# Batch 0's norms in a fused attention and MLP kernel: transposed scores, inverse norms on ScalarE, squares summed on VectorE

## The chip, the cores and the metric

One NeuronCore of a Trainium2 chip. The metric is the device time of one execution in microseconds (us), as the median of several runs; lower is better. The engines are TensorE (PE in the profile; its weight loads are PEld), VectorE (DVE), ScalarE (ACT), GpSimd (POOL), which issues most loads here, and SyncE (SP).

## The reference

Two steps. The first is an attention over channels: for each of 4 batches, q and k (6080 rows, 256 channels) are scaled so that each channel has norm 1 over its rows; the 256x256 matrix of scores is their product over the rows, a softmax goes over it, and v is multiplied by the result. The second is an MLP with a squared relu.

```python
B, N, C = (4, 6080, 256)            # q, k, v; float32
qn = q / (norm(q, axis=1) + 1e-06)
kn = k / (norm(k, axis=1) + 1e-06)
s = kn.transpose(0, 2, 1) @ qn / tau          # tau = 1
a = softmax(s, axis=-1)                       # (sum + 1e-9 below)
x = (v @ a).reshape(24320, 256)
r = maximum(x @ w_in, 0)                      # w_in: 256 x 2048
out = (s_moe * r * r + b_moe) @ w_out         # w_out: 2048 x 256, out float32
```

## The kernel before

Everything is in fp16 with fp32 sums. The kernel forms `wa = a @ w_in` for each batch (a 256x2048 matrix), so that the main stream is `h = wa^T v^T`, relu, square, and the product with `w_out`. The main stream runs over groups of 512 rows, 16 steps each; the scores of the next batch are formed in small pieces between its steps. Batch 0 has no stream to hide behind: its q and k are loaded, its scores, norms and softmax are done, and only then does the stream begin.

The rows of a batch come in chunks of up to 512 rows (128 partitions, JC = 4 rows each). For batch 0 there are 11 chunks of 512 and two short ones (256 and 192 rows); the k rows of the two short ones are loaded before their q rows.

```python
    def mm(self, c, j):                       # the Gram product of q and k
        ...
            po(nc.tensor.matmul(
                self.s_ps[:, ch, :],
                kc[:np_, j, ts(ch, P)],
                qc[:np_, j, :],
        ...
    def norm_ops(self, c):
        # squares of k on ScalarE, of q on VectorE, then two folds on VectorE:
        #   4 rows to 2 (128x1024 out), 2 rows to 1 (128x512 out)
        ...
            if last and (self.b == 0 or c == 0 or c == len(self.chunks) - 1):
                for rows in self.rows:
                    rows.append((st["f", half], np_, 1))
        ...
        def into_first():                     # later batches: a DMA adds the fold to chunk 0's
            dst, src = self.rows[0][0][0][:np_], st["f", 1][:np_]
            po(nc.gpsimd.dma_start(out=dst, in_=src, accum_op=ALU.add))
        ...
    def add_norms(self, arrays=(0, 1), last=False):
        # sums over the partitions: products of 128x128 pieces of the folds with a column of ones
        ...
                po(nc.tensor.matmul(self.n_ps[a][:, ch : ch + 1], t[:np_, a, j, ts(ch, P)],
                                    ones16[:np_, 0:1], ...))
```

From the sums to the softmax (`finish_ops`): a root as exp(0.5 ln), an added eps and a reciprocal; then in batch 0 a scaling of the scores by k's inverse norm, a transpose on TensorE in fp32, and the exps with q's inverse norm as scale. In later batches the scaled scores are split into two fp16 halves, transposed by DMA and joined.

```python
        def root(out, sums):
            po(nc.scalar.activation(out=out, in_=sums, func=AF.Ln, bias=tiny))
            po(nc.scalar.activation(out=out, in_=out, func=AF.Exp, scale=0.5))
        def recip(a=None):
            ...
            po(nc.vector.tensor_scalar_add(out=nrm, in0=nrm, scalar1=EPS))
            po(nc.vector.reciprocal(out=r, in_=nrm))
        def scale():                          # batch 0
            for ch in range(CH):
                po(nc.vector.tensor_scalar_mul(
                    out=st["s"][:, ch], in0=self.s_ps[:, ch],
                    scalar1=st["r"][:, 1, ch : ch + 1]))
        def split(part): ...                  # later batches: "hi", "lo", each with two DMA transposes
        def join(): ...
        def turn(): ...                       # batch 0: nc.tensor.transpose with ident32
        def exps(j):
            po(nc.scalar.activation(
                out=st["e"][:, j, :], in_=st["t"][j], func=AF.Exp,
                scale=st["r"][:, 0, j : j + 1]))
```

The opening, in program order. Fillers (`keep_busy`) are products whose result nobody reads; they keep TensorE's activity up between the loads.

```python
    FILL = {-9: 2, -8: 2, -7: 2, -6: 4, -5: 4, -4: 4, -3: 2}     # 128x512 fp16 each
    for c in range(NCH0 - 2):
        ops = g0.norm_ops(c)
        if c >= NCH0 - 3:
            g0.add_norms()
        for j in range(g0.chunks[c][2]):
            g0.mm(c, j)
        ...                                   # fillers, then the squares and folds
    ops = [g0.norm_ops(c) for c in (NCH0 - 2, NCH0 - 1)]
    g0.add_norms()
    for k_squares, _, into_rows in ops:
        k_squares()
        into_rows()
    fin[0]()                                  # k's norm
    fin[1]()                                  # k's reciprocal
    keep_busy(NFILL, ...)
    for c in (NCH0 - 2, NCH0 - 1):
        ops[c - NCH0 + 2][1]()                # q's squares
        for j in range(g0.chunks[c][2]):
            g0.mm(c, j)
    ...                                       # q's norm, scaling, reciprocal, transpose
    transpose_v(0)
    keep_busy(2, w_in16[:, 0, :P], w_in16[:, 0, :NW])
    for f in fin[6:12]:                       # exps, row sums, first pieces of wa
        f()
```

Of the kernel before, what the change touches and what calls it, by code (L numbers as in the profile page):

```python
# [16 lines left out]
def kernel(  # L17
# [32 lines left out]
    SHIFT = 3  # L50
    assert CH == 2 and FT == 16
# [14 lines left out]
    sq_pool = pool("sq_pool", 2)  # L66
    f3_pool = pool("f3_pool", 13)
# [41 lines left out]
    class Gram:  # L109
# [32 lines left out]
        def mm(self, c, j):  # L142
            qc, kc = self.tiles[c]
            _, np_, jc = self.chunks[c]
            for ch in range(CH):
                po(nc.tensor.matmul(  # L146
                    self.s_ps[:, ch, :],
                    kc[:np_, j, ts(ch, P)],
                    qc[:np_, j, :],
                    start=(c == 0 and j == 0 and ch == 0),  # L150
                    stop=(c == len(self.chunks) - 1 and j == jc - 1 and ch == CH - 1),
                    skip_group_check=True,
                ))

        def norm_ops(self, c):
# [4 lines left out]

            def squares(a, js):
                def f():
                    if "sq" not in st:
                        st["sq"] = sq_pool.tile([P, 2, JC, C], FP16, tag="sq", name="sq")
                    if a == 0:
# [7 lines left out]
            def fold(half, arrays, last):  # L173
                def f():
# [10 lines left out]
                    if last and (self.b == 0 or c == 0 or c == len(self.chunks) - 1):  # L185
                        for rows in self.rows:
                            rows.append((st["f", half], np_, 1))
                return f

            def into_first():  # L190

                dst, src = self.rows[0][0][0][:np_], st["f", 1][:np_]
                po(nc.gpsimd.dma_start(out=dst, in_=src, accum_op=ALU.add))  # L193

            def unfolded():
                for rows in self.rows:
                    rows.append((st["sq"], np_, jc))
# [5 lines left out]
            if jc == 2:  # L203
# [4 lines left out]
            return ops + [into_first] if self.b > 0 and 0 < c < len(self.chunks) - 1 else ops  # L208

        def add_norms(self, arrays=(0, 1), last=False):  # L210

            if self.b > 0:

                self.n_all = x_tile[0][:, 1, : 2 * CH].rearrange("p (a c) -> p a c", a=2)
                self.n_ps = [self.n_all[:, 0], self.n_all[:, 1]]
            for a in arrays:
                first = self.n_ps[a] is None
                if first:
                    self.n_ps[a] = ps_o.tile([P, 2, C], FP32, tag="o_ps", name="n_ps")[:, 0, :CH]
                todo = [(t, np_, j, ch) for t, np_, jc in self.rows[a] for j in range(jc)  # L220
                        for ch in range(CH)]
                self.rows[a].clear()
                for i, (t, np_, j, ch) in enumerate(todo):
                    po(nc.tensor.matmul(self.n_ps[a][:, ch : ch + 1], t[:np_, a, j, ts(ch, P)],
                                        ones16[:np_, 0:1], start=(first and i == 0),
                                        stop=(last and i == len(todo) - 1),
                                        skip_group_check=True))

        def finish_ops(self):
# [3 lines left out]
            def root(out, sums):  # L233

                po(nc.scalar.activation(out=out, in_=sums, func=AF.Ln, bias=tiny))
                po(nc.scalar.activation(out=out, in_=out, func=AF.Exp, scale=0.5))

            def norms(a=None):

                if "r" not in st:  # L240
                    st["nrm"] = sm_pool.tile([P, 2, CH], FP32, tag="nrm", name="nrm")
                    st["r"] = sm_pool.tile([P, 2, CH], FP32, tag="rnrm", name="rnrm")
                if a is None:
                    self.add_norms(last=True)
                    root(st["nrm"], self.n_all)
                else:
                    self.add_norms((a,), last=True)
                    root(st["nrm"][:, a], self.n_ps[a])

            def recip(a=None):  # L250
                own = slice(0, 2) if a is None else slice(a, a + 1)
                nrm, r = st["nrm"][:, own], st["r"][:, own]
                po(nc.vector.tensor_scalar_add(out=nrm, in0=nrm, scalar1=EPS))
                po(nc.vector.reciprocal(out=r, in_=nrm))
                if inv_tau != 1.0 and a != 1:
                    po(nc.vector.tensor_scalar_mul(
                        out=st["r"][:, 0], in0=st["r"][:, 0], scalar1=inv_tau))

            def scale():
                st["s"] = sm_pool.tile([P, CH, C], FP32, tag="sm_s", name="sm_s")  # L260
                for ch in range(CH):
                    po(nc.vector.tensor_scalar_mul(
                        out=st["s"][:, ch], in0=self.s_ps[:, ch],
                        scalar1=st["r"][:, 1, ch : ch + 1]))


            def split(part):
                st[part] = sm_pool.tile([P, CH, C], FP16, tag=f"s_{part}", name=f"s_{part}")
                rk = st["r"][:, 1]
                if part == "hi":  # L270
                    po(nc.vector.tensor_mul(
                        st["hi"], self.s_ps, rk[:, :, None].broadcast_to((P, CH, C))))
                else:
                    for ch in range(CH):
                        po(nc.vector.scalar_tensor_tensor(
                            out=st["lo"][:, ch], in0=self.s_ps[:, ch], scalar=rk[:, ch : ch + 1],
                            op0=ALU.mult, in1=st["hi"][:, ch], op1=ALU.subtract))
                st[part + "T"] = sm_pool.tile([P, CH, C], FP16, tag=f"t_{part}", name=f"t_{part}")
                for ch in range(CH):
                    po(nc.sync.dma_start_transpose(  # L280
                        out=st[part + "T"][:, :, ts(ch, P)], in_=st[part][:, ch, :]))

            def join():
                t_sb = sm_pool.tile([P, CH, C], FP32, tag="sm_s", name="t_sb")
                po(nc.vector.tensor_add(t_sb, st["hiT"], st["loT"]))
                st["t"] = [t_sb[:, j, :] for j in range(CH)]

            def turn():

                st["t"] = [h_tile("t_ps")[:, 0, :C], self.bank("t_ps", CH, C)[:, 0, :]]  # L290
                for ch in range(CH):
                    for j in range(CH):
                        po(nc.tensor.transpose(
                            st["t"][j][:, ts(ch, P)], st["s"][:, ch, ts(j, P)], ident32))

            def exps(j):
                if j == 0:
                    st["e"] = sm_pool.tile([P, CH, C], FP16, tag="eT", name="eT")
                po(nc.scalar.activation(
                    out=st["e"][:, j, :], in_=st["t"][j], func=AF.Exp,  # L300
                    scale=st["r"][:, 0, j : j + 1]))
# [53 lines left out]
            if self.b == 0:  # L355
                front = [lambda: norms(1), lambda: recip(1), lambda: norms(0),
                         scale, lambda: recip(0), turn]
            else:
                front = [norms, recip]
                front += [lambda: split("hi"), lambda: split("lo"), join]  # L360
# [46 lines left out]
    ident32 = consts.tile([P, P], FP32)  # L407
    make_identity(nc, ident32)
# [12 lines left out]
    nc.vector.memset(tiny, 1e-30)  # L421
    for c in range(NDIRECT):
        g0.load(c)
        g0.cast(c)
    for c in range(NDIRECT, len(g0.chunks) - 2):
        g0.load(c)

    for parts in ((0,), (1,)):
        for c in range(len(g0.chunks) - 2, len(g0.chunks)):
# [7 lines left out]
    load_w_in(0, NW)  # L437
    load_v(0)
    load_w_in(NW, 2 * NW)
# [20 lines left out]
    NFILL = 3  # L460
    FILL = {-9: 2, -8: 2, -7: 2, -6: 4, -5: 4, -4: 4, -3: 2}

    def keep_busy(n, w, x):

        idle_ps = h_tile("idle_ps")[:, 0, :]
        for _ in range(n):
            po(nc.tensor.matmul(idle_ps, w, x, start=True, stop=True, skip_group_check=True))

    fin = g0.finish_ops()
    for c in range(NCH0 - 2):  # L470
        ops = g0.norm_ops(c)
        if c >= NCH0 - 3:
            g0.add_norms()
# [3 lines left out]
        if fill:  # L477
            keep_busy(fill, g0.tiles[c][1][:, 0, :P],
                      g0.tiles[c][0][:, :2, :].rearrange("p j c -> p (j c)"))
# [3 lines left out]
    ops = [g0.norm_ops(c) for c in (NCH0 - 2, NCH0 - 1)]  # L483
    g0.add_norms()
    for k_squares, _, into_rows in ops:
        k_squares()
        into_rows()
    fin[0]()
    fin[1]()
    keep_busy(NFILL, g0.tiles[NCH0 - 3][1][:, 0, :P],  # L490
              g0.tiles[NCH0 - 3][0][:, :2, :].rearrange("p j c -> p (j c)"))
    for c in (NCH0 - 2, NCH0 - 1):
        ops[c - NCH0 + 2][1]()
        for j in range(g0.chunks[c][2]):
            g0.mm(c, j)
    for f in fin[2:5]:
# [404 lines left out]
```

## Time and profile before

The time is 718.97 us, the median of three runs from 718.74 to 719.09. The profiled execution spans 717.2 us.

| engine | busy us | share | instructions |
|---|---|---|---|
| TensorE | 698.9 | 97% | 7479 |
| VectorE | 626.1 | 87% | 882 |
| ScalarE | 536.5 | 75% | 579 |
| GpSimd | 109.8 | 15% | 189 |

| stretch, us | TensorE busy | VectorE busy | ScalarE busy |
|---|---|---|---|
| 0 to 10 | 1.87 | 1.98 | 2.81 |
| 10 to 20 | 7.44 | 8.23 | 6.79 |
| 20 to 30 | 6.72 | 8.48 | 4.20 |
| 30 to 40 | 9.26 | 6.12 | 5.07 |
| 40 to 50 | 10.00 | 7.52 | 8.48 |

The page gives busy time over the whole run first; an engine with a high share need not be the one that is waited for, so the shares are read by stretch. A line of the timeline has the start and the length in us, the engine, the line of the kernel, the operation with what it writes and reads, and in brackets how long the engine had been idle and what ended that. Lines with x2 or more are several instructions merged. The length of a matmul counts from its start to its modelled end and overlaps the next one's; the distance between starts tells the rate.

### The profile page before, as it was taken

The numbers are of one execution on the slowest core, as the hardware profiler recorded it, in microseconds if no ns is written. First come the engines' busy times: TensorE is split into PE (matmuls) and PEld (weight loads), VectorE is DVE, ScalarE is ACT, GpSimd is POOL, SyncE is SP. The second block draws the span as 40 slices with busy tenths as digits, with TensorE's granted clock in tenths as the row PEclk, the third lists the DMA queues.
The fourth block names the chain that finished last, engine by engine and source line by source line (L and its number), as shares of the span: only waits on it lengthen the run. The fifth ranks groups of instructions, "written<-read, shape, count | busy, mean of one in ns | idle before, by whom it ended". The sixth has DMA issues, their size and how long they took to land.

```text
span 717.2 us, 17629 instructions
## 1 busy us (share of the span) xinstructions
PE 698.9 (97%) x7479; PEld 504.6 (70%) x7479; DVE 626.1 (87%) x882; ACT 536.5 (75%) x579; POOL 109.8 (15%) x189
## 2 busy tenths in 40 slices
PE   4799999999999999999999999999999999999998
PEld 2556777776677777777677777777668777777777
DVE  4879999999789999999889899999887888888886
ACT  4479877787777777777777778777877777777875
POOL 4532332101201222111110222110000000000000
PEclk9999999999999999999999999999999999999999
DMA  9999998647556879443972877944423333321201
GB/s 236 207 259 172 159 170 137 111 108 129 119 107 114 144 133 145 108 93 83 154 151 57 141 138 124 154 90 86 105 63 75 93 71 74 97 60 46 83 30 74
DMA packets 89790, 84.25 MB, mean 117 GB/s; under 512 B 59664, under 2 KB 64848, under 8 KB 89712
## 3 DMA queue, kind: packets, MB, share of 16 engines
q0 software_dynamic: 26064, 43.40, 37.5%
q1 hardware_dynamic: 63072, 38.43, 21.5%
q8 instruction: 58, 0.95, 0.6%
q10 hardware_dynamic: 576, 1.31, 0.5%
q14 instruction: 20, 0.16, 0.1%
HBM read 78.91 MB, written 24.90 MB: 145 GB/s over the span
## 4 chain that ended last, share of the span: by engine, by line
PE 93%; DMA 4%; DVE 1%; ACT 1%; POOL 1%; issue 0%; POOLq 0%; ACTq 0%
PE h_ps L641 45%; PE o_ps L809 40%; PE s_ps L146 4%; DMA qk<-in_q_dram 3%; PE wa_ps L326 2%; DMA v<-in_v_dram 1%; PE o_ps L713 1%; PE o_ps L687 0%; POOL qk L130 0%; ACT r L651 0%; DVE o_sb L669 0%; DVE S L737 0%; DVE sq L166 0%; DVE S L735 0%; DVE S L739 0%
## 5 line engine op out<-in xcount | busy, mean ns | idle before, releaser
L651 ACT ACTIVATE r<-h_ps 128x1024 f16<-128x1024 f32 (+1 forms) x384 | 388.4, 1014 | 153.4 <-PE h_ps L641 150.9
L641 PE MATMUL h_ps<-vT,wa 128*128 128x512 f16 (+7 forms) x1632 | 452.1, 364 | 0.1
L809 PEld LDWEIGHTS <-S 128*128 128x128 f16 x2944 | 198.0, 98 | 85.0 <-issue 0.9
L809 PEld LDWEIGHTS <-g 128*128 128x128 f16 x2208 | 155.0, 98 | 74.1
L664 DVE TENSOR_TENSOR g<-r 128x2048 f16<-128x2048 f16 (+2 forms) x150 | 174.8, 1165 | 14.6 <-ACT r L651 14.5
L809 PE MATMUL o_ps<-T,S 128*128 128x128 f16 x2208 | 183.3, 219 | 0.1
L641 PEld LDWEIGHTS <-wa 128*128 128x128 f16 x1632 | 135.9, 98 | 20.6 <-ACT wa L319 0.3
L809 PE MATMUL o_ps<-w_out,g 128*128 128x128 f16 x1472 | 134.2, 219 | 0.2 <-DVE u L669 0.2
L669 DVE SCALAR_TENSOR_TENSOR o_sb<-o_ps,s_out,u 128x256 f32<-128x256 f32 x138 | 66.5, 482 | 47.1 <-PE o_ps L809 44.5
L662 ACT ACTIVATE g<-r 128x1024 f16<-128x1024 f16 (+1 forms) x97 | 100.4, 1035 | 0.2
L146 PE MATMUL s_ps<-qk 128*128 128x256 f16 (+1 forms) x384 | 69.6, 281 | 14.0 <-ACT qk L137 8.7
L379 POOL DMA_DIRECT2D v<-in_v_dram x48 | 31.3, 656 | 263.5 <-DMA vT<-v 209.6
L669 DVE SCALAR_TENSOR_TENSOR u<-o_ps,s_out,rowconst 128x256 f32<-128x256 f32 x138 | 66.0, 478 | 0.0
L809 PE MATMUL o_ps<-w_out,S 128*128 128x128 f16 x736 | 63.5, 219 | 0.0
L809 PE MATMUL o_ps<-N,g 128*128 128x128 f16 x736 | 63.4, 219 | 0.0
L193 POOL DMA_DIRECT2D f<-f x30 | 26.3, 877 | 225.6 <-DVE f L182 172.0
L169 ACT ACTIVATE sq<-qk 128x1024 f16<-128x1024 f16 (+3 forms) x49 | 50.4, 1033 | 10.0 <-DMA qk<-in_k_dram 6.7
L737 DVE TENSOR_TENSOR S<-S,g 128x2048 f16<-128x2048 f16 (+1 forms) x47 | 56.4, 1201 | 1.3
L735 DVE TENSOR_TENSOR S<-g 128x2048 f16<-128x2048 f16 (+1 forms) x47 | 56.1, 1193 | 0.0
L741 DVE TENSOR_TENSOR S<-g,S 128x2048 f16<-128x2048 f16 x46 | 56.0, 1217 | 0.0
L739 DVE TENSOR_TENSOR S<-g 128x2048 f16<-128x2048 f16 x46 | 55.9, 1216 | 0.0
L146 PEld LDWEIGHTS <-qk 128*128 128x128 f16 (+1 forms) x384 | 32.8, 101 | 20.1 <-DVE qk L136 8.0
(74 smaller groups left out, 314.9 us busy)
## 6 DMA issues: line engine op xcount, KB each, us to landing
out_dram<-o_sb SPq DMA_DIRECT2D x46, 512.0 KB, 3.0
v<-in_v_dram POOLq DMA_DIRECT2D x47, 256.0 KB, 4.7
qk<-in_k_dram POOLq DMA_DIRECT2D x42, 256.0 KB, 6.1
qk<-in_q_dram POOLq DMA_DIRECT2D x42, 256.0 KB, 7.2
f<-f POOLq DMA_DIRECT2D x30, 128.0 KB, 3.1
vT<-v SPq DMA_TRANSPOSE x182, 3.2
w<-in_moe_w_out_dram POOLq DMA_DIRECT2D x4, 512.0 KB, 11.3
raw<-in_k_dram SPq DMA_DIRECT2D x2, 512.0 KB, 6.4
```

Of the source, the lines that this page charges most:

```text
L146: po(nc.tensor.matmul(self.s_ps[:, ch, :], kc[:np_, j, ts(ch, P)], qc[:np_, j, :], start=(c == 0 and j == 0 and ch == 0), stop=(c == len(s ...
L169: po(nc.scalar.activation(out=st["sq"][:np_, 1, js, :], in_=kc[:np_, js, :], func=AF.Square))
L641: po(nc.tensor.matmul(dst, wa[:, ci, ts(m, P)], src, start=(ci == 0), stop=(ci == CH - 1), skip_group_check=True))
L651: po(nc.scalar.activation(out=r16[:, :, i % 2, :n], in_=h_tiles.pop((g, i))[:, :, :n], func=AF.Relu))
L662: po(nc.scalar.activation(out=dst, in_=src, func=AF.Square))
L664: po(nc.vector.tensor_mul(dst, src, src))
L669: po(nc.vector.scalar_tensor_tensor(out=dst, in0=src, scalar=s_out, op0=ALU.mult, in1=add, op1=ALU.add))
L735: po(nc.vector.tensor_add(T[1], A21, A22))
L737: po(nc.vector.tensor_sub(T[2], T[1], A11))
L739: po(nc.vector.tensor_sub(T[3], A11, A21))
L741: po(nc.vector.tensor_sub(T[4], A12, T[2]))
L809: po(nc.tensor.matmul(st[name][:, j, :], a()[:, i, ts(j, P)], w[:, i, :], start=first, stop=last, skip_group_check=True))
```

## The change

It changes how batch 0 gets from its squares to the first product of the main stream, and how later batches get from their scores to the softmax.

- The scores are formed transposed (q is the stationary operand, k the moving one). So neither the transpose on TensorE in batch 0 nor the split, the DMA transposes and the join in later batches are needed; k's inverse norm then lies along the free axis, as a row repeated on all partitions.
- k's sums are formed as such rows (a 128x128 matrix of ones against the 256 channels), and both inverse norms are done on ScalarE: ln, exp(0.5 .), ln(. + eps), exp(-.).
- The folds of batch 0's chunks 1 to 9 are added to chunk 0's on VectorE, where TensorE summed each before.
- Three late chunks where there were two: the k rows of chunks 10 to 12 are loaded before their q rows, and k's norm is finished before the late Gram products.
- Fillers are few, and fp32. v's first group is loaded before w_in, of which the first 512 columns come in two pieces.
- In later batches the ScalarE steps stand some steps of the stream apart.

```diff
-                    kc[:np_, j, ts(ch, P)],
-                    qc[:np_, j, :],
+                    qc[:np_, j, ts(ch, P)],
+                    kc[:np_, j, :],
 ...
-                    if last and (self.b == 0 or c == 0 or c == len(self.chunks) - 1):
+                    if last and (c == 0 or self.b > 0 and c == len(self.chunks) - 1):
 ...
             def into_first():
                 dst, src = self.rows[0][0][0][:np_], st["f", 1][:np_]
-                po(nc.gpsimd.dma_start(out=dst, in_=src, accum_op=ALU.add))
+                if self.b == 0:
+                    po(nc.vector.tensor_add(dst, dst, src))
+                else:
+                    po(nc.gpsimd.dma_start(out=dst, in_=src, accum_op=ALU.add))
 ...
+            def unfolded(a):                  # late chunks: k's squares are added on VectorE
+                if a == 0:
+                    self.rows[0].append((st["sq"], np_, jc))
+                    return
+                ...
+                po(nc.vector.tensor_add(dst, dst, src))
 ...
-            return ops + [into_first] if self.b > 0 and 0 < c < len(self.chunks) - 1 else ops
+            return ops + [into_first] if 0 < c < len(self.chunks) - 1 else ops
 ...
+                if a == 1:
+                    row = t[:np_, j] if len(t.shape) == 3 else t[:np_, 1, j]
+                    po(nc.tensor.matmul(self.n_ps[1], ones16[:np_, :], row, ...))
 ...
+            def inverse(a):
+                def part(i):
+                    ...
+                    func, kw = [(AF.Ln, dict(bias=tiny)), (AF.Exp, dict(scale=0.5)),
+                                (AF.Ln, dict(bias=eps)), (AF.Exp, dict(scale=-1.0))][i]
+                    po(nc.scalar.activation(out=r, in_=r if i else self.n_ps[a], func=func, **kw))
 ...
+                    po(nc.vector.tensor_mul(st["t"][:, js], self.s_ps[:, js],
+                                            rk[:, None, :].broadcast_to((P, n, C))))
 ...
-    load_w_in(0, NW)
     load_v(0)
+    load_w_in(0, 2 * P)
+    load_w_in(2 * P, NW)
 ...
-    FILL = {-9: 2, -8: 2, -7: 2, -6: 4, -5: 4, -4: 4, -3: 2}
+    FILL = {-8: 1, -6: 1, -5: 2, -4: 2}
+    def fill_32(n):
+        keep_busy(raw32[:, 0, 0, 0, :P], raw32[:, 0, 1, :n, :])
 ...
+    for a in (1, 0):
+        g0.add_norms(a)
+    ops = {c: g0.norm_ops(c) for c in late}
+    for c in late:
+        k_squares, _, into_rows = ops[c]
+        k_squares()
+        into_rows(1)
+    norms_k()
+    for f in inverse_k:
+        f()
+    fill_32(1)
+    for c in late:
+        ops[c][1]()
+        ops[c][2](0)
         for j in range(g0.chunks[c][2]):
             g0.mm(c, j)
+        if c == NCH0 - 1:
+            norms_q()
+        else:
+            g0.add_norms(0)
+    for f in inverse_q:
+        f()
+    scale_s()
     transpose_v(0)
 ...
-    FIN = (0, 3, 5, 7, 15, 17, 19, 22)
+    FIN = (0, 3, 5, 7, 9, 16, 18, 19, 20, 21, 22, 26, 28, 31)
 ...
-        fin_len = 54
+        fin_len = 58
```

## The prediction

> **What bounds the kernel now.** I read the busy shares of the page first, then the table of busy time by stretch, then the chain that ended last, and last the timeline of the first 40 us, engine by engine. Page, first part; the chain by line; and the stretch 75 to 700 us:
>
> ```profile
> PE 698.9 (97%) x7479; PEld 504.6 (70%) x7479; DVE 626.1 (87%) x882; ACT 536.5 (75%) x579; POOL 109.8 (15%) x189
> ...
> PE h_ps L641 45%; PE o_ps L809 40%; PE s_ps L146 4%; DMA qk<-in_q_dram 3%; PE wa_ps L326 2%; DMA v<-in_v_dram 1%; PE o_ps L713 1%; PE o_ps L687 0%; POOL qk L130 0%; ACT r L651 0%; DVE o_sb L669 0%; DVE S L737 0%; DVE sq L166 0%; DVE S L735 0%; DVE S L739 0%
> ...
> 75.00:700.00 625.00, 624.98 (x6837) 453.50 (x6836) 557.81 (x759) 477.24 (x502) 80.62 (x131) 1.00 0.56 107
> ```
>
> From 75 to 700 us TensorE is busy 624.98 of 625.00 us: nothing that VectorE or ScalarE saves there can shorten the run unless TensorE's own work changes. What is left to win or lose is the opening, before the first product of the main stream (h_ps), where TensorE waits for batch 0's softmax. So the view that decides is the timeline of 28 to 39 us; TensorE, VectorE and ScalarE (columns: start us, length us, engine, line, operation):
>
> ```profile
> 28.52 0.69 DVE L166 TENSOR_TENSOR sq<-qk 128x1024 f16<-128x1024 f16 x1 [0.61 <-DMA qk<-in_q_dram]
> 32.97 0.25 PE L224 MATMUL n_ps<-ones,f 128*128 128x1 f16 x4 [0.23 <-DVE f L182]
> 33.47 0.26 ACT L235 ACTIVATE nrm<-n_ps,tiny 128x2 f32<-128x2 f32 x1 [0.34 <-PE n_ps L224]
> 33.76 0.20 ACT L236 ACTIVATE nrm<-nrm 128x2 f32<-128x2 f32 x1
> 34.00 0.24 DVE L253 TENSOR_SCALAR nrm<-nrm 128x2 f32<-128x2 f32 x1 [1.08 <-ACT nrm L236]
> 36.43 0.84 ACT L299 ACTIVATE eT<-t_ps,rnrm 128x256 f16<-128x256 f32 x2 [0.50 <-PE t_ps L293]
> 37.44 0.24 PE L309 MATMUL r_ps<-parts,eT 128*128 128x1 f16 x4
> 38.60 0.60 PE L641 MATMUL h_ps<-vT,wa 128*128 128x512 f16 x2
> ```
>
> The loads of q and k arrive every 2.5 us per chunk (Gram products of chunks 4 to 8 start at 15.96, 18.52, 20.97, 23.52, 25.98). At 28.52 VectorE has caught up and waits 0.61 us for q. From there the chain is: last full chunk's fold on VectorE, norm sums on TensorE (32.97), ScalarE (33.47), VectorE, exps (36.43 to 37.27), sums (37.44), first h_ps at 38.60.
>
> That VectorE has caught up by then is not a given. Chunks 1 to 7 find it without a pause; one chunk reads
>
> ```profile
> 16.34 0.69 DVE L166 TENSOR_TENSOR sq<-qk 128x1024 f16<-128x1024 f16 x1
> 17.12 0.69 DVE L182 TENSOR_TENSOR f<-sq 128x1024 f16<-128x1024 f16 x1
> 17.85 0.42 DVE L182 TENSOR_TENSOR f<-f 128x512 f16<-128x512 f16 x1
> 18.19 0.68 DVE L166 TENSOR_TENSOR sq<-qk 128x1024 f16<-128x1024 f16 x1
> ```
>
> Start to start this is 1.85 us; over chunks 1 to 7 (squares at 12.62 and 23.77) it is 11.15 / 6 = 1.86 us. The squares of chunk 4 begin 18.19 - 15.96 = 2.2 us behind their data, and the lag shrinks by 2.5 - 1.86 = 0.65 us a chunk. It is gone only at chunk 8.
>
> **What the Trainium skill says.** "VectorE: DVE Perf Modes", section "The DRAIN you can't avoid": the next operation does not start until the pipe is empty, so the count of operations is what costs. The trace agrees: the starts above are 0.73 to 0.78 us apart for operations of 0.69 us. "ScalarE: Activation LUTs", section "What ACT_TABLE_LOAD costs": an ACTIVATE takes some 280 ns with a pointer bias, 186 ns without, plus 0.833 ns per element. With 2 elements the trace has 0.26 and 0.20 us; for 256 elements I estimate from the page 0.49 and 0.40 us, and the exps of the trace, 128x256, take 0.42 to 0.47. "TensorE: Matmul & The Clock Gate", Part 1: after a window of about 3.4 us with little work the array runs at half its clock. Here the first eight Gram products at 7.05 us last 418 ns each and those from 15.96 on 272 ns, so both states occur in this opening; no gap in the trace of before is long enough to show the way back.
>
> **The change, part by part.**
>
> 1. Squares summed on VectorE. Chunks 1 to 9 of batch 0 each get one more 128x512 fp16 add (0.42 us by the row of the same shape; it depends on the fold before it, so I count 0.45). Forty small norm products leave TensorE (1.14 us at 30.27), which were off the path. The period per chunk becomes 1.86 + 0.45 = 2.31 us, still under 2.5, but the lag now shrinks by only 0.2 us a chunk. From chunk 1 at 12.62: 12.62 + 9 x 2.31 = 33.4 us for the end of chunk 9's add. In before, chunk 9 was folded at 30.46. **This is the step I rest on: 3 us of VectorE lag that before did not have.**
>
> 2. k's last rows first, three late chunks. The k rows of chunks 10 to 12 land before their q rows, so the k norm could start early: but their sums stand in VectorE's queue behind chunk 9. An add of 0.42, then twice a square (0.40, from the 128x512 row) and an add (0.42): 5 x 0.40 = 2.0 us, end at 35.4. The same sum in before was ready at 32.9.
>
> 3. Norm rows and inverse norms on ScalarE. Norm product and hand-over as before (32.97 to 33.47) 0.45 us: 35.85. Four dependent ACTIVATEs on 128x256: 0.47 + 0.41 + 0.47 + 0.41 plus three hand-overs of 0.03 = 1.85 us: 37.7. In exchange the fp32 transposes (0.74 us), the additions of eps and the reciprocals (0.17 to 0.24 us each) leave.
>
> 4. TensorE meanwhile, in order behind the k norm product (35.65): one fp32 filler (0.43, as the 128x256 fp32 product at 62.8 us took), 16 Gram products at 0.108 = 1.73, 16 one-column norm products at about 0.025 = 0.4: 38.2, with latency 38.4. Then q's four small ACTIVATEs, 0.26 + 0.20 + 0.26 + 0.20 + 0.1 = 1.0: 39.4. The two scalings on VectorE (0.88) lie beside them. Exps 0.84: 40.3. From end of exps to the first h_ps before took 38.60 - 37.27 = 1.33 us: first h_ps at 41.6, that is **3.0 us later**.
>
> 5. Fillers. Before had 23 of 512 columns beside the q and k loads, now there are five fp32 ones (three of 0.43, two of 0.86 us). After chunk 9's pair, about 30.3 us, TensorE waits for VectorE till 33.4 and again till 35.4, with some five small products between. If the clock falls to half, part 4 takes up to 2.2 us more, less what is regained when it comes back: I count 1.3 us at a chance of one half.
>
> 6. v before w_in, and w_in in two pieces: v lands some 1.2 us earlier than the 36.5 of before. It would help if the exps came earlier; with these at 40 us it lies in slack.
>
> 7. Later batches. The high and low halves, their DMA transposes and the join go (about 2.2 us of VectorE per batch: 0.68 + 0.87 + 0.69), one scaling comes; eight ACTIVATEs come for two, some 2.4 us of ScalarE per batch, spread over 31 steps. Both engines have idle time (89% and 76% in the stretch above). TensorE: eight one-column products (0.2 us) become two of 256 columns and four of one, 0.32 us: 0.1 x 3 = 0.3 us more.
>
> Sum: 718.97 + 3.0 + 0.65 + 0.3 = 722.9. Since part 1 may be too harsh, I take 722.3.
>
> **Rivals.** (a) No lag: VectorE keeps up (the adds run faster, or the early chunks start sooner). Then k's norm runs while the last q lands, and the path is last q, its norm, four small ACTIVATEs, exps: with q in by about 33.2 the exps could start near 35.9 instead of 36.43, and v and w_in, landing by 36, allow it. That makes 718.3 to 718.7. For it speaks the intent and 2.31 < 2.5; against it the unbroken VectorE run from 12.6 to 25 us. (b) The lag plus a cold array: 724 to 725. For it speaks the 5 us of near idleness; against it that some small products lie in it and that the window, by the same section of the skill, is free-running. (c) ScalarE's longer chains in later batches hold the relus up and starve TensorE, 1 to 3 us over three batches. Against: in-order ScalarE waits for h_ps 151 us in total, and squares of 1.03 us already stand between its relus without a TensorE wait. (d) The relief of VectorE speeds the main stream: against it 624.98 of 625.
>
> **Range and chances.** Lag without cold clock gives about 722.2, with it 723.5, no lag 718.5. I give the lag four chances in five. Predicted 722.3 us, range 718.7 to 725.0. Two per cent is 14.4 us, out of reach of an opening of 38.6 us: faster by over 2% 0.005, within 2% 0.985, slower by over 2% 0.01.
>
> **What would show it.** In the profile after: VectorE with no idle time before the squares of chunks 8 and 9 and chunk 9's add ending near 33.4; k's first 128x256 Ln near 35.9; exps ending near 40.3; the first h_ps near 41.6; Gram products of the late chunks at 272 ns (warm) or some 418 (cold); TensorE still without gaps from 75 to 700 us. It is wrong if VectorE is seen waiting for q at chunk 8 or 9, or if k's inverse norm is done before the last q product.

## The result, and the profile after

The changed kernel takes 730.26 us (median of 5 runs, 729.93 to 731.01) against 719.01 us: 1.0159 times the time before, with a 95% interval of 1.0147 to 1.0172. It is slower by 11.25 us. The prediction had the sign, but 3.3 us.

The busy shares of the page after:

```profile
PE 698.3 (96%) x7417; PEld 503.3 (69%) x7417; DVE 626.3 (86%) x876; ACT 542.1 (74%) x599; POOL 110.1 (15%) x188
```

And the stretch 75 to 700 us from the table of busy time by stretch (the stretch, its length, then busy time and instructions of PE, PEld, DVE, ACT, POOL, granted clock, DMA share, GB/s):

```profile
75.00:700.00 625.00, 620.25 (x6756) 449.27 (x6755) 550.45 (x740) 478.57 (x520) 81.67 (x133) 1.00 0.58 105
```

Total busy time of TensorE is the same to 0.6 us; what is new is idle time. And it is not only in the opening: of the 625 us in which TensorE had been idle for 0.02 us, it is now idle for 4.75. The list of waits of TensorE says for what. These three rows (in all us, times, longest) have no counterpart of their size in the list of before:

```profile
PE o_ps L803 <- ACT r L266: 4.0, 6, 0.9
PE n_ps L246 <- DVE f L202: 3.4, 1, 3.4
PE n_ps L246 <- DVE sq L217: 1.6, 1, 1.6
```

The first row is the surprise: six times (two per later batch) a product of the main stream, o_ps, waits for ScalarE's ln of the norms. The other two are in the opening, as is a fourth, 1.2 us in two waits for the exps.

To place the loss I compared the start of every h_ps product in the two traces. The first comes 43.34 - 38.60 = 4.74 us later. From there to the last group the distance grows to 10.34 us, with a step up at each later batch's norms, and the profiled spans differ by 728.1 - 717.2 = 10.9 us, so some 0.6 us more lie after the last product. So: opening 4.7, later batches 5.6, end 0.6.

The opening after, VectorE (one chunk, then the end of the sums), TensorE and ScalarE:

```profile
24.46 0.68 DVE L174 TENSOR_TENSOR sq<-qk 128x1024 f16<-128x1024 f16 x1
25.24 0.69 DVE L190 TENSOR_TENSOR f<-sq 128x1024 f16<-128x1024 f16 x1
25.97 0.42 DVE L190 TENSOR_TENSOR f<-f 128x512 f16<-128x512 f16 x1
26.43 0.42 DVE L202 TENSOR_TENSOR f<-f,f 128x512 f16<-128x512 f16 x1
26.77 0.68 DVE L174 TENSOR_TENSOR sq<-qk 128x1024 f16<-128x1024 f16 x1
...
33.38 0.42 DVE L202 TENSOR_TENSOR f<-f,f 128x512 f16<-128x512 f16 x1
...
35.30 0.42 DVE L217 TENSOR_TENSOR sq<-sq 96x512 f16<-96x512 f16 x1
```

```profile
33.86 0.27 PE L246 MATMUL n_ps<-f,ones 128*128 128x256 f16 x1 [3.36 <-DVE f L202]
...
35.78 0.61 PE L246 MATMUL n_ps<-sq,ones 128*128 128x256 f16 x2 [1.62 <-DVE sq L217]
36.18 1.06 PE L450 MATMUL idle_ps<-raw 128*128 128x256 f32 x2
37.03 1.90 PE L148 MATMUL s_ps<-qk 128*128 128x256 f16 x8
...
43.34 0.60 PE L635 MATMUL h_ps<-vT,wa 128*128 128x512 f16 x2
```

```profile
36.43 0.47 ACT L266 ACTIVATE r<-n_ps,tiny 128x256 f32<-128x256 f32 x1 [5.56 <-PE n_ps L246]
...
40.23 0.26 ACT L266 ACTIVATE r<-n_ps,tiny 128x2 f32<-128x2 f32 x1 [1.89 <-PE n_ps L250]
...
41.32 0.91 ACT L287 ACTIVATE eT<-sm_t,r 128x256 f16<-128x256 f32 x2
```

The chunk's period on VectorE is 26.77 - 24.46 = 2.31 us, no row between 10 and 35 us shows a wait for q, and the last of chunk 9's adds ends at 33.8. TensorE waits 3.36 us for it, then 1.62 us for the late sums, and comes out of it slow: eight Gram products take 1.90 us where the kernel before has

```profile
33.94 1.04 PE L146 MATMUL s_ps<-qk 128*128 128x256 f16 x8
```

The main stream at the first later batch's norms (the norm products, then ScalarE's queue, then TensorE):

```profile
148.60 0.38 PE L246 MATMUL o_ps<-f,ones 128*128 128x256 f16 x2
...
149.46 1.02 ACT L645 ACTIVATE r<-h_ps 128x1024 f16<-128x1024 f32 x1
...
150.38 1.05 ACT L656 ACTIVATE g<-r 128x1024 f16<-128x1024 f16 x1
...
151.32 1.02 ACT L645 ACTIVATE r<-h_ps 128x1024 f16<-128x1024 f32 x1
...
152.23 0.48 ACT L266 ACTIVATE r<-o_ps,tiny 128x256 f32<-128x256 f32 x1
...
152.76 0.55 PE L803 MATMUL o_ps<-T,S 128*128 128x128 f16 x7 [0.87 <-ACT r L266]
```

The norm products are done at 149.0, but the ln that reads them runs at 152.23, behind two relus and a square in ScalarE's queue. TensorE stands still for 0.87 us and goes on 0.05 us after the ln has ended. Why should a product of the main stream wait for it? The product with `w_out` is done as seven products of half the size (Strassen's scheme), each in sixteen matmuls, of which seven go into a step of the stream. The first, third, fifth and seventh are summed in one half of the PSUM tile named X; the code puts the norms into its other, unused half. The third product is being written when the ln is due. No data pass from the ln to that product, yet the program has a wait on ScalarE ahead of it. I read it so: a write that stands behind a read of the same tile in the program waits for it, whichever half each touches, and from the ln's place in the program until ScalarE has done it the tile is closed to TensorE. No run gave the norms a tile of their own, which would test this directly; the first three experiments move the read instead.

The kernel before reads its norms from the same half of X, and there too the ln stands ahead of writes of the third product:

```profile
147.09 0.59 PE L641 MATMUL h_ps<-vT,wa 128*128 128x512 f16 x2
147.27 0.26 ACT L235 ACTIVATE nrm<-o_ps,tiny 128x4 f32<-128x4 f32 x1
147.58 0.50 PE L809 MATMUL o_ps<-T,S 128*128 128x128 f16 x6
```

But ScalarE gets to it 0.04 us after the norm products and has done it at 147.53, while TensorE is busy with two h_ps products; the next product of X starts 0.05 us later, without a pause. A read among the writes costs nothing as long as its engine gets to it in time.

### The profile page after: what moved, and what is told of

It reads as the page before. It is cut to its first block, busy times and chain, and to the rows that moved or that the text cites. A ratio compares the mean times of both kernels' runs of the same rounds, so it can differ in the third digit from the quotient of the medians.

```text
span 728.1 us, 17499 instructions
## 1 busy us (share of the span) xinstructions
PE 698.3 (96%) x7417; PEld 503.3 (69%) x7417; DVE 626.3 (86%) x876; ACT 542.1 (74%) x599; POOL 110.1 (15%) x188
## 4 chain that ended last, share of the span: by engine, by line
PE 84%; DVE 9%; ACT 4%; issue 1%; DMA 1%; SPq 0%; DVEq 0%; ACTq 0%
PE h_ps L635 40%; PE o_ps L803 36%; PE s_ps L148 4%; DVE f L190 2%; PE wa_ps L314 2%; ACT r L645 2%; ACT g L656 1%; DVE sq L174 1%; DMA raw<-in_k_dram 1%; DVE g L658 1%; DVE S L731 1%; DVE o_sb L663 1%; ACT sq L177 1%; PE o_ps L707 1%; DVE S L733 1%
## 5 line engine op out<-in xcount | busy, mean ns | idle before, releaser
L177 ACT ACTIVATE sq<-qk 128x1024 f16<-128x1024 f16 (+1 forms) x47 | 49.2, 1051 | 8.7 <-DVE f L190 8.3
```

Source lines behind the costliest of these rows:

```text
L177: po(nc.scalar.activation(out=st["sq"][:np_, 1, js, :], in_=kc[:np_, js, :], func=AF.Square))
```

## The experiments

Each kernel was timed against the kernel before on one chip; the differences below are to 730.26 us for the changed kernel and 719.0 to 719.2 us for the kernel before.

### The ln of later batches moved later

```diff
-    FIN = (0, 3, 5, 7, 9, 16, 18, 19, 20, 21, 22, 26, 28, 31)
+    FIN = (0, 5, 7, 9, 11, 16, 21, 22, 23, 24, 25, 28, 30, 33)
```

> The changed kernel with only the later batches' first ln of each norm moved two and three steps of the stream LATER (for k from 3 to 5 steps after the norm products, for q from 2 to 5). Theory A, the held PSUM tile: in the changed kernel the ln is issued while TensorE still has products of the third Strassen product to write into the tile whose other half holds the norms, so these wait for ScalarE; moved behind the last of them, the ln has until the fifth product, and the wait is gone although ScalarE is asked later. Expected: TensorE's idle time on ScalarE's ln from 4.0 us to under 0.5, time 725 us (730.3 less some 5.2). Theory B, ScalarE's load (eight longer ln and exp per batch between the relus hold TensorE up): the same ScalarE work remains, the time stays at 730.

Measured: 725.51 us, ratio to before 1.0088 (1.0073 to 1.0103). The wait of o_ps for ScalarE's ln is gone from the list of waits; the stretch 75 to 700 us:

```profile
75.00:700.00 625.00, 624.21 (x6812) 452.67 (x6810) 554.53 (x745) 483.50 (x526) 81.89 (x134) 1.00 0.58 106
```

TensorE gets back 4 us of busy time in it, while ScalarE does no less than in the changed kernel (483.50 against 478.57 us busy). So ScalarE's added load is not the cause; the place of the read is. By the medians 4.75 us of the 11.25 are this. The profile says the same apart from the opening: from the first h_ps to the last group the kernel now loses 0.66 us on the kernel before, where it lost 5.59. That is 0.9 us more than the six waits themselves; where these 0.9 us go is open. The opening of this execution is 1.28 us longer than in the profile of the changed kernel (first h_ps at 44.62), though its code is the same: q and k came 0.6 us later, and TensorE was slow for longer (last section).

### The ln moved earlier

```diff
-    FIN = (0, 3, 5, 7, 9, 16, 18, 19, 20, 21, 22, 26, 28, 31)
+    FIN = (0, 1, 5, 7, 9, 16, 17, 19, 20, 21, 22, 26, 28, 31)
```

> The changed kernel with the later batches' first ln moved EARLIER (for k from 3 steps to 1 step after the norm products, for q from 2 to 1). Theory A: ScalarE's queue at that point still holds a relu and a square, and the third product starts some two steps later, so the wait shrinks but stays: for k from 0.87 to some 0.4 us, for q unchanged at 0.46 as no ScalarE work stood between; idle time 2.4 to 3.2 us instead of 4.0, time 728.7 to 729.3. That is worse than moving it later (725.5). If only the distance from the norm product mattered, sooner would be the better side: under 725.

Measured: 729.73 us, ratio 1.0146 (1.0131 to 1.0161). The idle time is 3.0 us of the expected 2.4 to 3.2:

```profile
PE o_ps L803 <- ACT r L266: 3.0, 6, 0.6
```

The median lies some 0.4 us above the expected range. Of its four executions two lie in it (729.00 us at a mean granted clock of TensorE of 0.998, 729.24 at 0.995), and the two in which TensorE was slow for longer lie above it (730.22 and 730.58, both at 0.992). Moving the read closer to the norm products helps little, since a relu and a square stand before it in ScalarE's queue anyway; moving it two or three steps further away, behind the last of the third product's sixteen matmuls, ends the wait. Distance is not what counts, but which writes stand behind the read and how late ScalarE gets to it.

### The same delay put into the kernel before

```diff
                     self.add_norms(last=True)
-                    root(st["nrm"], self.n_all)
 ...
-                front = [norms, recip]
+                front = [norms, lambda: root(st["nrm"], self.n_all), recip]
 ...
-    FIN = (0, 3, 5, 7, 15, 17, 19, 22)
+    FIN = (0, 3, 5, 7, 9, 17, 19, 21, 24)
 ...
-        fin_len = 54
+        fin_len = 58
```

> The kernel before with one thing of the change alone: in the later batches the norm products stand four steps earlier and the roots (ln, exp) three steps after them, as in the changed kernel; nothing else is changed, so ScalarE's work is the same two short ACTIVATEs a batch. Theory A, the held PSUM tile: TensorE waits for the ln once per batch, some 0.8 us and a restart, in all 2 to 2.8 us: time 721 to 721.8. Theory B, ScalarE's load: nothing was added, the time stays at 719.0.

Measured: 722.66 us, ratio 1.0043 (1.0029 to 1.0058). TensorE's list of waits:

```profile
PE o_ps L808 <- ACT nrm L235: 2.0, 3, 0.7
```

Three waits of up to 0.7 us, one per later batch, appear in a kernel that has none of the rest of the change. The norm products are done at 144.35 us, but the ln stands behind a square and a relu in ScalarE's queue and runs at 147.61, where it ran 0.04 us after them before. The first h_ps comes at 38.76, and by the last group the products are 2.94 us behind the kernel before, 2.78 of them after the first h_ps, where 2 to 2.8 were expected. The profiled execution is the fastest of the four (721.84 us); the median is 0.9 us above the expected range, and why is open.

### Batch 0's folds summed by TensorE again

```diff
-                    if last and (c == 0 or self.b > 0 and c == len(self.chunks) - 1):
+                    if last and (self.b == 0 or c == 0 or c == len(self.chunks) - 1):
-            return ops + [into_first] if 0 < c < len(self.chunks) - 1 else ops
+            return ops + [into_first] if self.b > 0 and 0 < c < len(self.chunks) - 1 else ops
```

> The changed kernel with batch 0's folds summed by TensorE again (one row product per chunk for k, two one-column products for q) instead of by nine adds on VectorE. Theory A, VectorE's lag: VectorE finishes chunk 9 near 30.5 us instead of 33.8, k's first ln starts near 32.9 instead of 36.4, and the first h_ps comes near 39 to 40 instead of 43.3: time 726 to 727. Theory B, the longer chain of ScalarE (four wide steps for k, four small ones for q) and the cold array make the delay: the first h_ps stays beyond 42, time 729 to 730.

Measured: 725.95 us, ratio 1.0092 (1.0077 to 1.0107). VectorE, TensorE and ScalarE in its opening:

```profile
28.59 0.69 DVE L174 TENSOR_TENSOR sq<-qk 128x1024 f16<-128x1024 f16 x1 [0.59 <-DMA qk<-in_q_dram]
...
30.36 1.26 PE L246 MATMUL n_ps<-f,ones 128*128 128x256 f16 x10
31.45 0.64 PE L250 MATMUL n_ps<-ones,f 128*128 128x1 f16 x20
...
33.40 0.47 ACT L266 ACTIVATE r<-n_ps,tiny 128x256 f32<-128x256 f32 x1 [2.52 <-PE n_ps L246]
...
39.08 0.81 PE L635 MATMUL h_ps<-vT,wa 128*128 128x512 f16 x2
```

VectorE waits for q again, TensorE does all sums in 1.7 us in a gap that it had anyway, k's ln starts 3.0 us earlier, and the first h_ps comes at 39.08 instead of 43.34. With 2.31 us of work for every 2.5 us of loads VectorE was never over its budget, yet this costs 4.3 us, some 1.4 of them by way of the slow array that the next experiment takes out.

### The gap filled

```diff
+    for _ in range(4):
+        fill_32(2)
     for a in (1, 0):
         g0.add_norms(a)
+    for _ in range(2):
+        fill_32(2)
```

> The changed kernel with six more fp32 fillers of 512 columns, four ahead of the wait for VectorE's sums and two behind it, so that TensorE does not idle from 30.5 to 35.8 us. Theory A, the array falls to half its clock in that gap: the late Gram products last 272 ns instead of some 418, the last of them ends 1.2 to 1.5 us earlier, the first h_ps comes near 42.0, time about 729. Theory B, the clock is no matter because the chain runs over VectorE and ScalarE: time 730.3, first h_ps at 43.3.

Measured: 728.63 us, ratio 1.0128 (1.0111 to 1.0145), 1.6 us less than the changed kernel. The late Gram products last 272 ns in the median (269 to 273), against up to 421 ns in the changed kernel:

```profile
37.13 1.04 PE L148 MATMUL s_ps<-qk 128*128 128x256 f16 x8
```

The first h_ps comes at 42.58, in an execution whose loads and VectorE run some 0.7 us later than in the changed kernel's (Gram products of chunk 9 at 29.28 against 28.59, its add done at 34.47 against 33.80); so 1.4 us of that opening are the slow array, with VectorE's sums as late as ever.

### VectorE's sums put into the kernel before

```diff
-                    if last and (self.b == 0 or c == 0 or c == len(self.chunks) - 1):
+                    if last and (c == 0 or self.b > 0 and c == len(self.chunks) - 1):
-                po(nc.gpsimd.dma_start(out=dst, in_=src, accum_op=ALU.add))
+                if self.b == 0:
+                    po(nc.vector.tensor_add(dst, dst, src))
+                else:
+                    po(nc.gpsimd.dma_start(out=dst, in_=src, accum_op=ALU.add))
-            return ops + [into_first] if self.b > 0 and 0 < c < len(self.chunks) - 1 else ops
+            return ops + [into_first] if 0 < c < len(self.chunks) - 1 else ops
-        if c >= NCH0 - 3:
-            g0.add_norms()
```

> The kernel before with one thing of the change alone: batch 0's folds of chunks 1 to 10 added to chunk 0's on VectorE. Theory A, VectorE's lag: its period per chunk goes from 1.86 to 2.3 us, it no longer catches up with the loads, chunk 10 is folded near 35.7 instead of 32.9 us and the first h_ps comes near 41.5 instead of 38.6: time 722. Theory B, VectorE has room because 2.3 is under the 2.5 us of the loads: time 719.1.

Measured: 723.83 us, ratio 1.0061 (1.0044 to 1.0077), more than the 722 expected. TensorE:

```profile
36.39 0.26 PE L227 MATMUL n_ps<-ones,f 128*128 128x1 f16 x4 [3.67 <-DVE f L194]
...
37.97 1.91 PE L146 MATMUL s_ps<-qk 128*128 128x256 f16 x8
...
43.28 1.87 PE L329 MATMUL wa_ps<-w_in,eT 128*128 128x256 f16 x8
44.95 0.63 PE L642 MATMUL h_ps<-vT,wa 128*128 128x512 f16 x1
```

VectorE's last add ends at 36.3 us, 0.6 later than expected, as its first square began 0.56 us later in this execution (10.25 against 9.69). What I had left out is the array: after 3.67 us of waiting it is slow and stays so up to the first h_ps (1.87 us for eight products that took 1.03). How much that costs differs: the profiled execution is the slowest of the four (725.82 us, mean granted clock 0.993); the others took 724.42 (0.995), 723.24 and 723.11 (both 0.998), all above 722.

### Both repairs, and one step on

Both: the first and the fourth diff of this section together. One step on: in addition the norm products of q's last two chunks ahead of the last chunk's Gram products.

```diff
+        if c == NCH0 - 1:
+            norms_q()
         for j in range(g0.chunks[c][2]):
             g0.mm(c, j)
-        if c == NCH0 - 1:
-            norms_q()
-        else:
+        if c == NCH0 - NLATE:
             g0.add_norms(0)
```

> The changed kernel with both repairs at once: later batches' first ln moved behind the third product, and batch 0's folds summed by TensorE. If the two causes are separate, their gains add: 730.3 less 4.8 less 4.3 is 721.2, no TensorE wait on ScalarE's ln and the first h_ps near 39.1. If they share a part, it stays at 722 to 724. If they are all that the change cost, it reaches the kernel before, 719.1; the traces so far leave some 2 us beyond them (opening 0.5, later batches 0.2 each, the end 0.6), so 721 is expected, not 719.

> As the last, and the norm products of q's last two chunks stand ahead of the last chunk's Gram products, so that ScalarE's four small steps for q begin while TensorE finishes the scores. If q's norm ends the opening now, its ln starts at some 35.5 us instead of 36.0 and the first h_ps comes 0.4 us earlier: time 720.7. If the scores end it (scaling on VectorE after the last Gram product), nothing is gained: 721.1.

Measured: both 721.03 us, ratio 1.0026 (1.0015 to 1.0036); one step on 720.88 us, ratio 1.0021 (1.0012 to 1.0030). The two repairs gain 9.23 us, their single gains 4.75 + 4.31 = 9.06: they are separate causes, and together they are all of the loss but 1.8 us. The further step moves q's ln in the profile (it starts 2.12 us after k's, where it was 2.56 in the run with TensorE's sums), but the first h_ps comes at 39.18 against 39.16, in an execution whose loads ran some 0.45 us later, and the gain of 0.15 us in the medians is within the intervals. Neither beats the kernel before.

## Why the prediction was wrong

**The wait in the later batches was denied, and that is the step that failed.** Part 7 gave the later batches 0.3 us, for more columns of norm products, and rival (c) allowed 1 to 3 us for ScalarE holding up relus; TensorE was to be "still without gaps from 75 to 700 us". The measured growth from the first h_ps to the last group is 5.6 us, of which moving the two reads of each batch removes 4.9. That TensorE was busy 624.98 of 625 us meant that nothing could be won there; it did not mean that nothing could be lost. The argument against (c), that ScalarE waits for h_ps 151 us in total, was true and beside the point: not the relus were late but a read of a PSUM tile that TensorE wanted to write. I had read that the norms lie in the unused half of X, and that the ln was moved three steps away from them, and did not ask who writes the tile in between, nor what stands ahead of the ln in ScalarE's queue. The kernel's order of steps had it: the seven products begin in a group's fourth step, the norm products come in its fifth and k's ln in its eighth, when the third product has just begun and a relu stands ahead of the ln.

**Part 1, VectorE's lag, was right**: 2.31 us per chunk, as predicted, and chunk 9's add ending at 33.8 against 33.4. Parts 2 and 3 came 0.3 to 0.6 us late as well (late sums at 35.7 against 35.4; k's ln at 36.43 against 35.85), mostly carried over from part 1, whose first square began 0.35 us later in this execution (10.04 against 9.69), and from the two norm products at half clock; the hand-over that part 3 counts as 0.45 us is 0.50 by its own lines.

**Part 5, the cold array (rival (b)), was real and was counted by half only.** Eight Gram products took 1.90 us, and the run with fillers won 1.4 us of the opening, against 1.3 counted at a chance of one half. Parts 1 to 5 with the cold array in full make 3.0 + 1.3 = 4.3 us; 4.74 was measured, with the exps ending at 42.2 us instead of part 4's 40.3. The opening alone would have given 719.0 + 4.7 = 723.7 us. The 0.6 us at the end stand in no part.

**Rival (a)**, no lag, is refuted by the trace. **Rival (d)**, a faster main stream through a lighter VectorE, likewise: with both repairs nothing is gained over before.

**The reading that VectorE's operations start only when the one before is through** held for the two pairs that the prediction names (starts 0.78 and 0.73 us apart at 0.69 us). The last two of its four lines show another case: the next chunk's square starts at 18.19, before the fold of 17.85 + 0.42 = 18.27 has ended. The periods that part 1 rests on are measured, and stand.

What stays open is the last 1.8 us. Between the profile with both repairs and that of before (2.1 us in their spans) the opening is 0.56 us longer, the stream from there to the last group 0.90 and the end 0.65. No run takes these apart.

## What to carry to other kernels

When an intermediate is parked in a corner of a buffer that another engine is filling, ask what the program lets that engine do between the reader's issue and its turn in its queue: the place of the read among the writer's instructions and the work ahead of it in its own queue count, not its distance from the write, and a later read can be the cheaper one. An engine with 2.31 us of work per 2.5 us of data still fails if it begins the stretch behind: what counts is when the lag is gone. And a gap that opens on TensorE just ahead of a chain is paid twice, once as waiting and once in products at the slow clock.

## What the runs showed of the hardware

After some 5 us with only 0.3 us of products (30.5 to 35.8 us) TensorE's 128x256 products last up to 421 ns instead of 272. "TensorE: Matmul & The Clock Gate", Part 1, of the Trainium skill describes this fall; the trace before had no gap of that length once its products had begun. Fillers in the gap kept it away. When the clock comes back differs between executions of the same opening: in the profile of the changed kernel the products last 270 ns again from 38.98 us on, 3.2 us after dense work began at 35.78; in that of the run with the ln moved later only from 41.1 us on, 4.7 us after it began at 36.38.

Nor did the fall need a gap of 5 us. In the profile of the same run the Gram products at 24 us are slow as well:

```profile
24.20 1.89 PE L148 MATMUL s_ps<-qk 128*128 128x256 f16 x8 [1.51 <-DMA qk<-in_q_dram]
```

In the 3.5 us ahead of them TensorE had worked 1.05 us and never paused for more than 1.51 us. Four of the seven profiles with the changed kernel's few fillers show such a stretch between 23 and 28 us, and none of the three with the fillers of before.

In the profile of the changed kernel, and of each of the six that were made from it, one packet of the instruction queue lies in the last microsecond, after the last store:

```profile
q14 instruction: 1, 0.01, 0.5%
```

The kernel before has none there, nor have the two made from it. From TensorE's last product to the end of the span it takes 3.8 us in each of the seven profiles with the packet and 3.2 in each of the three without; that the one makes the other was not tried.
